# A Fourier transform and two feed-forward layers on one core: layer 1 begins with two token blocks on a quarter of its weights, and the weight conversion changes form

## The chip, the cores and the metric

The program runs on one core of one Trainium2 chip, in one launch. Its engines are TensorE (PE; PEld is its weight load), VectorE (DVE), ScalarE (ACT), GpSimd (POOL) and SyncE (SP, which here only issues DMAs). The metric is device time in microseconds; less is better.

## The reference, cut to what matters

```python
batch, seq, dim = (4, 3008, 256)          # x: float32
n_tokens, d_model, d_ff = (12032, 256, 2048)  # weights float32

X = np.fft.fft(x, axis=1); X = np.fft.fft(X, axis=2); x1 = X.real
h = x1 @ w_in          # layer 1
g = np.maximum(h, 0.0) ** 2
x2 = g @ w_out
h = x2 @ w_in2         # layer 2
y = (h * np.cos(h)) @ w_out2
```

The weights reach the kernel as 8-byte floats (they are drawn and then scaled in double precision), so each must be turned into two 12-bit-rounded float32 parts, "hi" and "lo".

## The kernel before, in words

Every matmul is done in three products of the two parts (hi by hi, hi by lo, lo by hi), so a stationary 128x128 tile meets 512 moving columns three times. The transform uses symmetries: tokens are handled in 6020 pairs, 1505 per batch; the pairs of all batches stand in one row and are cut into 12 blocks of 512 (the last has 388). A batch's input comes in three pieces of rows (`load_x`), each of which is **folded**: sums and differences on VectorE (`fold_a`, `fold_eo`, `fold_b`), then split into hi (`fold_hi`, ScalarE) and lo (`fold_lo`). `transform` multiplies the folded rows with tables of sines and cosines (six pieces, loaded once, kept to the end of the transforms), in four jobs per batch (cos and sin, part 0 and part 1); `finish` adds and splits the result and stores it to DRAM as z. The Fourier transform along the other axis is multiplied into `w_in` (`dft_w1`, `split_w1`).

**Layer 1** goes block by block; a block has 16 steps, one for each tile f of 128 of the 2048 hidden units. In a step TensorE makes h (`l1_mm1`, L462, 6 matmuls), VectorE makes s = sum and difference of the pair (`l1_add`, L469 and two of L215), ScalarE does relu, square and the hi part (`l1_act`, L479 to L482), GpSimd the lo part gl (`l1_lo`, L490, two halves), and three steps later TensorE adds to the block's result in PSUM (`l1_mm2`, L502, 12 matmuls). h has two PSUM tiles; the result of a block takes two more (acc), which `l1_out` empties after the 16th step. **Layer 2** (L535 to L586) does the same kind of work in 24 half blocks of 8 steps.

**Conversions.** `from_f64` works on 128 x 512 weights: two 32-bit words each. In the window of layer 1's first block there are 14 of them: six for `w_in` (pieces (1,0) to (3,1); a chunk of two gives four tiles f) and eight for `w_out` (keys 0, 2, ... 14, two tiles f each). Each has on VectorE a mask (L164), a merge (L167), a rest (L170), a guarded hi part (L180) and a power (L183). In ten of them ("shared", by the table `SHARED`) ScalarE and GpSimd make the lo part (L175, L188 on GpSimd); in the other four two more instructions on VectorE do (L177, L190). 16 conversions for layer 2's weights run late in layer 1, all on VectorE.

The first batch's input is folded and its part 0 transformed before layer 1; part 1 in its first steps. Layer 1's first block needs a new chunk of `w_in` every four steps and a new key of `w_out` every two. Batch 1 is folded in steps 11 to 24 and its z is needed by block 2, which reaches into batch 1, at step 32. x pieces of batches 1 to 3 go through the buffers A and B, which `l1_out` also uses.

**Order.** Each call is put into a list with a time in steps (`Order.at`), which the table `TIMES` may replace by name; the list is sorted and issued. An engine runs its instructions in that order and waits for semaphores; nothing is reordered on the chip. `FOLDS` says which of batch 0's first and last fold operations run on GpSimd ("P").

Of the kernel before, what the change touches and what calls it, by code (L numbers as in the profile page):

```python
# [89 lines left out]
def kernel(ctx: ExitStack, tc: tile.TileContext, x, x128, cs, tab0, tab1, w_in1, w_out1, w_in2, w_out2, out):  # L90
# [530 lines left out]
    def convert(t, key, st, fn, steps=(-0.5, 0, 0, 0)):  # L621
# [3 lines left out]
        def start():  # L625
            got.extend(fn(shared))
            for g in got[:4]:
                g()
# [253 lines left out]
```

## Time and profile before

| | |
|---|---|
| median of three runs | 1972.07 us (1969.3 to 1972.27) |
| the profiled execution | 1969.98 us, span 1968.2 us |
| busy share of the span | PE 96%, ACT 75%, DVE 72%, POOL 56% |
| layer 1's first step / 25th step / 49th step begins | 41.6 / 197.8 / 313.6 us |
| layer 2's first step begins | 928.5 us |

The profiled execution spends 1.8 us outside its span. Times in rows count from the span's start. A group of rows by line gives the busy time of all its instructions, the mean of one, and the idle time of the engine just before them with what ended it. `x12` is a count.

### The profile page before, as it was taken

How to read it: one execution, taken by the hardware profiler on the slowest of the kernel's cores; microseconds unless marked ns; L12 is line 12 of the kernel's file. 1: busy time of each engine (PE TensorE's matmuls, PEld its weight loads, DVE VectorE, ACT ScalarE, POOL GpSimd, SP SyncE). 2: the span in 40 equal slices, each digit the busy share in tenths (PEclk: the TensorE clock that was granted, in tenths of full speed). 3: DMA queues.
4: the chain of work that ended last, by engine and by line, in shares of the span. 5: the costliest groups of instructions: out<-in, count | busy, mean ns of one | idle time of the engine just before them, and what ended most of it. 6: DMA issues, size and time to landing. Idle time of an engine off the chain costs nothing.

```text
span 1968.2 us, 23258 instructions
## 1 busy us (share of the span) xinstructions
PE 1896.0 (96%) x8544; PEld 1575.4 (80%) x8544; DVE 1424.7 (72%) x1558; ACT 1472.3 (75%) x1519; POOL 1093.3 (56%) x716
## 2 busy tenths in 40 slices
PE   5688999999999999999999999999999999999999
...
GB/s 250 96 91 86 90 113 65 82 56 107 49 93 126 81 145 112 130 64 173 117 33 46 51 33 33 33 33 32 33 63 35 33 33 33 32 33 34 58 27 17
DMA packets 64389, 140.17 MB, mean 71 GB/s; under 512 B 7680, under 2 KB 19088, under 8 KB 64276
## 3 DMA queue, kind: packets, MB, share of 16 engines
...
q8 instruction: 67, 1.10, 0.2%
...
## 4 chain that ended last, share of the span: by engine, by line
PE 66%; DVE 11%; ACT 4%; issue 2%; DMA 0%; DVEq 0%; POOL 0%; ACTq 0%
PE acc L586 26%; PE h L535 17%; PE acc L502 9%; PE acc L535 8%; PE h L462 4%; DVE s L215 4%; DVE u L469 2%; ACT s L480 1%; ACT s L479 1%; DVE cvh L180 1%; DVE f L177 1%; PE h L290 1%; DVE f L170 1%; DVE ol L215 1%; ACT gh L482 1%
## 5 line engine op out<-in xcount | busy, mean ns | idle before, releaser
L574 POOL TENSOR_TENSOR gl<-r,gh 128x1024 fp32r<-128x1024 f32 (+1 forms) x189 | 446.4, 2362 | 539.6 <-ACT gh L567 468.1
L490 POOL TENSOR_TENSOR gl<-s,gh 128x512 fp32r<-128x512 f32 (+1 forms) x384 | 515.8, 1365 | 247.8 <-ACT gh L482 213.5
L549 DVE SCALAR_TENSOR_TENSOR r<-n,h 128x1024 f32<-128x1024 int32 (+1 forms) x129 | 154.7, 1199 | 214.5 <-ACT n L541 214.5
L479 ACT ACTIVATE s<-s 128x1024 f32<-128x1024 f32 (+1 forms) x192 | 199.6, 1040 | 137.2 <-DVE s L215 133.4
L215 DVE TENSOR_TENSOR s<-u,h 128x512 f32<-128x512 f32 (+1 forms) x384 | 242.8, 674 | 28.7 <-POOL inB L328 2.8
L541 ACT ACTIVATE n<-h 128x1024 int32<-128x1024 f32 (+1 forms) x129 | 130.4, 1011 | 155.2 <-PE h L535 155.2
L502 PE MATMUL acc<-gh,wbh 128*128 128x512 f32 (+1 forms) x768 | 238.3, 392 | 1.6 <-DVE ol L215 1.6
L549 DVE SCALAR_TENSOR_TENSOR r<-n,r 128x1024 f32<-128x1024 int32 (+1 forms) x192 | 232.7, 1212 | 6.6
L502 PE MATMUL acc<-gh,wbl 128*128 128x512 f32 (+1 forms) x768 | 235.7, 388 | 0.0
L502 PE MATMUL acc<-gl,wbh 128*128 128x512 f32 (+1 forms) x768 | 234.8, 387 | 0.0
L469 DVE SCALAR_TENSOR_TENSOR u<-zb,wc,h 128x512 f32<-128x512 f32 (+1 forms) x192 | 140.3, 731 | 127.7 <-PE h L462 125.3
L557 ACT ACTIVATE r<-r,halfpi 128x1024 f32<-128x1024 f32 (+1 forms) x192 | 218.4, 1138 | 6.2
L480 ACT ACTIVATE s<-s 128x1024 f32<-128x1024 f32 (+1 forms) x192 | 200.6, 1045 | 6.1
L482 ACT ACTIVATE gh<-s 128x1024 fp32r<-128x1024 f32 (+1 forms) x192 | 200.6, 1045 | 6.1
L556 ACT ACTIVATE r<-r 128x1024 f32<-128x1024 f32 (+1 forms) x192 | 198.2, 1032 | 6.7 <-DVE r L549 6.7
L586 PE MATMUL acc<-gh,wbl 128*128 128x512 f32 (+1 forms) x768 | 202.0, 385 | 0.0
L586 PE MATMUL acc<-gh,wbh 128*128 128x512 f32 (+1 forms) x768 | 202.0, 385 | 0.0
L586 PE MATMUL acc<-gl,wbh 128*128 128x512 f32 (+1 forms) x768 | 202.0, 385 | 0.0
L535 PE MATMUL h<-xh,wah 128*128 128x512 f32 (+1 forms) x516 | 198.8, 385 | 3.0 <-issue 1.5
L535 PE MATMUL h<-xl,wah 128*128 128x512 f32 (+1 forms) x516 | 198.5, 385 | 0.0
L535 PE MATMUL h<-xh,wal 128*128 128x512 f32 (+1 forms) x516 | 198.5, 385 | 0.0
L567 ACT ACTIVATE gh<-r 128x1024 fp32r<-128x1024 f32 (+1 forms) x192 | 197.1, 1027 | 0.3 <-DVE r L215 0.3
...
## 6 DMA issues: line engine op xcount, KB each, us to landing
...
```

What stands on the lines that cost most here:

```text
L215: nc.vector.tensor_tensor(out=out, in0=in0, in1=in1, op=op)
L479: nc.scalar.activation(s[:, :, :w], s[:, :, :w], AF.Relu)
L480: nc.scalar.activation(s[:, :, :w], s[:, :, :w], AF.Square)
L482: nc.scalar.activation(hi[:, :, :w], s[:, :, :w], AF.Copy)
L490: nc.gpsimd.tensor_tensor(out=lo[:, n, :w], in0=s[:, n, :w], in1=f32(hi)[:, n, :w], op=ALU.subtract)
L502: nc.tensor.matmul(accs[1, k][m][:, n, :w], wt, g[:, n, :w], start=f == 0 and i == 0, stop=f == NF - 1 and i == 2)
L535: nc.tensor.matmul(a[:, j, :w], st, mv[:, m, :w], start=m == 0 and q == 0, stop=m == 1 and q == 2)
L549: nc.vector.scalar_tensor_tensor(out=r[:, :, :w], in0=n[:, :, :w], scalar=-c, in1=src[:, :, :w], op0=ALU.mult, op1=ALU.add)
L556: nc.scalar.activation(r[:, :, :w], r[:, :, :w], AF.Abs)
L557: nc.scalar.activation(r[:, :, :w], r[:, :, :w], AF.Sin, bias=halfpi, scale=-1.0)
L574: e.tensor_tensor(out=lo[:, :, :w], in0=r[:, :, :w], in1=f32(hi)[:, :, :w], op=ALU.subtract)
L586: nc.tensor.matmul(accs[2, k][:, m, :w], w_out_t([c[part] for c in wo2], f, m), g[:, j, :w], start=f == 0 and q == 0, stop=f == NF - 1 and ...
```

## The change

The 1504 first pairs of a batch make three blocks of their own (512, 512, 480; the last batch 512, 512, 484), so that blocks follow batches. Layer 1 runs in **phases**: block 0 with tiles f 0 to 3, block 1 with f 0 to 3, block 2 with all 16, then block 1 and block 0 with f 4 to 15, then the others whole. After a phase that is cut short ScalarE copies the PSUM sums (`l1_part`), they go to DRAM, and come back (`load_part`) to be added in `l1_out`. Batch 1's z is needed at step 48 instead of 32, and its folding stands behind the conversions; x pieces of batches 1 to 3 are staged in the buffers of the tables, which are therefore loaded again for each batch (`reload_tab`, six pieces, GpSimd's DMA queue).

A conversion reads the same weights a second time, shifted by two bytes (`load_mid`, or in `load_cv`), so that the middle bits come out in a word of their own. `from_f64` then has on VectorE a guard (L171), a mask (L175), a merge (L179), a rest (L187 or L189), a power (L183) and the lo part (L196), ScalarE takes the absolute value before and the hi part after the merge, and nothing runs on GpSimd; the four earliest conversions read no shifted copy and keep a join (L192). Every step of a conversion or fold has its own time. Batch 0's fold is all on VectorE, its quarter sums moved behind part 0's transforms. Layer 2's conversions begin at step 101 (110 before), five steps each (four before). `TIMES` is a new table of 488 entries.

```diff
-BLOCKS = [(c, min(BLK, NPAIR - c)) for c in range(0, NPAIR, BLK)]
+BLOCKS = [(JB // 16 * 16 * b + c, min(BLK, (NPAIR - JB // 16 * 16 * b if b == B - 1 else JB // 16 * 16) - c))
+          for b in range(B) for c in range(0, JB, BLK)]
 NB = len(BLOCKS)
+PHASES = [(0, 0, FCH), (1, 0, FCH), (2, 0, NF), (1, FCH, NF), (0, FCH, NF)] + [(k, 0, NF) for k in range(3, NB)]
+SEQ = [(k, f) for k, f0, f1 in PHASES for f in range(f0, f1)]
...
-SHARED = {(3, 1): False, (2, 1): False, 0: False, 8: True, (0, 1): False, (0, 0): True, 4: True, (1, 1): False, (1, 0): True}
-FOLDS = {(2, 1): 'P', (0, 0): 'P', (0, 1): 'P', (1, 1): 'P', (1, 0): 'D', (2, 0): 'D'}
...
+FOLDS = {}
...
+    def shifted_in(w, k, col, n):
+        return w.bitcast(I16)[k * P:(k + 1) * P, 4 * col + 1:4 * (col + n) - 1]
+    def shifted_out(w, f, n):
+        return w.bitcast(I16)[f * P:(f + n) * P, 1:4 * D - 1].rearrange("(f p) m -> p f m", p=P)
...
+        def size():
+            got["a"] = buf("f64t", "f64t", I32, fft, 1, (P, BLK)) if sh is None else other
+            nc.scalar.activation(got["a"].bitcast(F32), w1.bitcast(F32), AF.Abs)
+        def guard():
+            a = got["a"].bitcast(F32)
+            v.tensor_scalar(out=a, in0=a, scalar1=TINY, scalar2=None, op0=ALU.max)
...
         def merge():
-            v.scalar_tensor_tensor(out=got["a"], in0=w1, scalar=-0x40000000, in1=got["a"], op0=ALU.bitwise_and, op1=ALU.bitwise_or)
+            a = got["a"]
+            v.scalar_tensor_tensor(out=a, in0=w1, scalar=-0x40000000, in1=a, op0=ALU.bitwise_and, op1=ALU.bitwise_or)
+            nc.scalar.activation(hi, a.bitcast(F32), AF.Copy)
...
+        def power():
+            v.tensor_scalar(out=got["a"], in0=got["a"], scalar1=-0x800000, scalar2=None, op0=ALU.bitwise_and)
 
...
-            v.tensor_scalar(out=w1, in0=w1, scalar1=0x1FF, scalar2=None, op0=ALU.bitwise_and)
+            if middle is None:
+                v.tensor_scalar(out=w1, in0=w1, scalar1=0x1FF, scalar2=None, op0=ALU.bitwise_and)
+            else:
+                v.tensor_scalar(out=middle, in0=middle, scalar1=0x1FFFFFF, scalar2=None, op0=ALU.bitwise_and)
...
-        def upper_part():
-            v.scalar_tensor_tensor(out=hi, in0=sizes.pop(key), scalar=SMALLEST, in1=got["a"].bitcast(F32), op0=ALU.is_ge, op1=ALU.mult)
-
-        def power():
-            v.tensor_scalar(out=got["a"], in0=hi.bitcast(I32), scalar1=-0x800000, scalar2=None, op0=ALU.bitwise_and)
-
...
+            r, unit = (w1.bitcast(F32), 2.0 ** -20) if middle is None else (middle, 2.0 ** -36)
+            v.scalar_tensor_tensor(out=lo, in0=r, scalar=unit, in1=got["a"].bitcast(F32), op0=ALU.mult, op1=ALU.mult)
+        return [size, guard, mask, merge, rest, power] + [join] * (middle is None) + [lower]
...
+    def reload_tab(i, t):
+        tabs[i][t] = buf(f"t{i}{t}", f"t{i}{t}", F32R, fft, 1, (P, 2, TW[i]))
+        load_tab(i, t)
...
+        return [mirrored] + [lambda i=i, fn=fn: fn(i) for fn, i in (
+            (eo, 0), (eo, 1), (half, 0), (half, 1), (hi, 0), (lo, 0), (quarter, 0), (quarter, 1), (hi, 1), (lo, 1))]
...
+    def load_mid(key, tag):
+        t = buf(tag, "mid", I32, fft, 1, (P, 2, TW[int(tag[1])])).rearrange("p h n -> p (h n)")
+        sh = t[:, :2 * BLK]
+        spare[key] = sh.rearrange("p (n t) -> p n t", t=2),
+        if isinstance(key, tuple):
+            c, k = key
+            nc.sync.dma_start(out=sh.bitcast(I16)[:, :4 * BLK - 2], in_=shifted_in(w_in1, k, c * FCH * P, BLK))
+        else:
+            nc.sync.dma_start(out=sh.bitcast(I16).rearrange("p (f n) -> p f n", f=2)[:, :, :4 * D - 2], in_=shifted_out(w_out1, key, 2))
...
+    def l1_part(k, m):
+        c, w = BLOCKS[k]
+        s = buf(f"t{m}{k}", "part", F32, fft, 1, (P, 2, TW[m]))[:, :, :BLK]
+        nc.scalar.activation(s[:, :, :w], accs[1, k][m][:, :, :w], AF.Copy)
+        part_dram[k, m] = dram.tile([P, 2 * BLK], F32, name=f"part{k}{m}")
+        nc.sync.dma_start(out=part_dram[k, m].rearrange("p (n w) -> p n w", n=2)[:, :, :w], in_=s[:, :, :w])
+    def load_part(k, m):
+        w = BLOCKS[k][1]
+        parts[k, m] = buf(f"{'BA'[m]}1", "ol", F32R)
+        nc.sync.dma_start(out=f32(parts[k, m])[:, :, :w], in_=part_dram[k, m].rearrange("p (n w) -> p n w", n=2)[:, :, :w])
 
     def l1_out(k, m):
...
-        tt(lo[:, :, :w], a[:, :, :w], f32(hi)[:, :, :w], ALU.subtract)
+        src = accs[1, k][m][:, :, :w]
+        hi = buf(f"{'BA'[m]}0", "oh", F32R)[:, :, :w]
+        if (k, m) in parts:
+            lo = parts.pop((k, m))[:, :, :w]
+            tt(f32(lo), src, f32(lo), ALU.add)
+            src = f32(lo)
+        else:
...
+    def staged(t):
+        return [buf(f"t{j // NT}{j % NT}", "inT", F32, fft, 1, (P, 2, TW[j // NT])).rearrange("p h n -> p (h n)")[:, :2 * BLK]
+                .rearrange("p (h n) -> p h n", h=2) for j in (2 * t, 2 * t + 1)]
...
+    KEYS = (0, 2, (1, 0), (1, 1), 4, (2, 0), (2, 1), 6, 8, (3, 0), (3, 1), 10, 12, 14)
+    t = 0.4
+    for n, key in enumerate(KEYS):
+        if n >= 2:
+            at(n * 1.5 - 1, lambda key=key, tag=f"t{n % 2}2": load_mid(key, tag), ("load_mid", key))
...
+            for t in range(NT):
+                at(start + gap * ((i * NT + t) // 2 + 1) + 0.1, lambda i=i, t=t: reload_tab(i, t), ("tab", b, i, t))
         for i, job in enumerate(JOBS):
-            def start(b=b, job=job):
+            def begin(b=b, job=job):
                 jobs[b, job] = ps_h.tile([P, 2, BLK], F32, name="h")
                 transform(job, jobs[b, job], lhs_of(b), P)
 
...
+    begins, i = {}, 0
+    for n, (k, f0, f1) in enumerate(PHASES):
+        begins[n] = i
+        if n == 1:
+            at(2.5, lambda k=k: load_zb(k, first["x"][1]), ("load_z", n))
+        elif n == 2:
+            at(4.2, lambda k=k: load_z(k), ("load_z", n))
+        elif n > 2 and PHASES[n - 2][0] != k:
+            at(max(i - 5.1, begins[n - 1] + 0.2), lambda k=k: load_z(k), ("load_z", n))
...
+            at(i + LAG + (1.25 if f == f0 else 0.3), lambda k=k, f=f, b=f == f0, e=f == f1 - 1: l1_mm2(k, f, b, e), ("mm2", i))
+            i += 1
         for m in range(2):
-            at(NF * (k + 1) + LAG - 0.55, lambda k=k, m=m: l1_out(k, m), ("out", k, m))
+            if f1 < NF:
+                at(i + LAG - 0.55, lambda k=k, m=m: l1_part(k, m), ("part", k, m))
+            else:
+                at(i + LAG - 0.55, lambda k=k, m=m: l1_out(k, m), ("out", k, m))
+                if f0:
+                    at(i + LAG - 2, lambda k=k, m=m: load_part(k, m), ("load_part", k, m))
 
     def open_late():
         fft_ctx.close()
...
```

Line numbers of the changed kernel follow in the rows below. **VectorE, the conversion of one pair of w_out tiles** early in layer 1: `wo` is the loaded weight, `mid` the shifted copy, `u` and `s` belong to `l1_add`, wbh and wbl are hi and lo. Before, a shared one (the lo part stands on GpSimd):

```order
L164 TENSOR_SCALAR f64t<-wo 128x512
L167 SCALAR_TENSOR_TENSOR f64t<-wo,f64t 128x512
L170 TENSOR_SCALAR wo<-wo 128x512
L469 SCALAR_TENSOR_TENSOR u_625<-zb,wc_96,h 128x512
L215 TENSOR_TENSOR s<-u_625,h 128x512 x2
L180 SCALAR_TENSOR_TENSOR wbh<-size,f64t 128x512
L183 TENSOR_SCALAR f64t<-wbh 128x512
```

and of the changed kernel, its steps after the guard:

```order
L175 TENSOR_SCALAR mid<-mid 128x512
L224 TENSOR_TENSOR wal<-h,wah 128x1024
L179 SCALAR_TENSOR_TENSOR mid<-wo,mid 128x512
L189 TENSOR_SCALAR mid<-mid 128x512
L536 SCALAR_TENSOR_TENSOR u_747<-zb,wc_96,h 128x512
L224 TENSOR_TENSOR s<-u_747,h 128x512 x2
L183 TENSOR_SCALAR mid<-mid 128x512
L196 SCALAR_TENSOR_TENSOR wbl<-mid 128x512
```

The hi part has left VectorE, the lo part has come to it, and one of the layer's `l1_add` groups stands between.

**VectorE, where batch 1's folding begins**: `inB` (before) and `inT` (now) are x pieces. Before, in the middle of the conversions:

```order
L469 SCALAR_TENSOR_TENSOR u_944<-zb,wc_96,h 128x512
L215 TENSOR_TENSOR s<-u_944,h 128x512 x2
L224 TENSOR_TENSOR inB_885<-inB_885,inB_886 128x1024
L164 TENSOR_SCALAR f64t<-wo 128x512
L167 SCALAR_TENSOR_TENSOR f64t<-wo,f64t 128x512
L170 TENSOR_SCALAR wo<-wo 128x512
L469 SCALAR_TENSOR_TENSOR u_1023<-zb,wc_96,h 128x512
L215 TENSOR_TENSOR s<-u_1023,h 128x512 x2
```

and now, after the last lo part of the last conversion:

```order
L536 SCALAR_TENSOR_TENSOR u_1443<-zb,wc_96,h 128x512
L224 TENSOR_TENSOR s<-u_1443,h 128x512 x2
L189 TENSOR_SCALAR mid<-mid 128x512
L183 TENSOR_SCALAR mid<-mid 128x512
L196 SCALAR_TENSOR_TENSOR wbl<-mid 128x512
L250 TENSOR_TENSOR inT<-inT 128x1024
L536 SCALAR_TENSOR_TENSOR u_1490<-zb,wc_96,h 128x512
L224 TENSOR_TENSOR s<-u_1490,h 128x512 x2
L224 TENSOR_TENSOR inT<-inT 128x512 x2
```

No fold of batch 1 now stands ahead of a conversion.

**GpSimd, the steps of the first blocks**: `gl` is `l1_lo`, wbl and wil the lo parts of weights, `t` a piece of the tables. Before:

```order
L175 TENSOR_TENSOR wo<-wo 128x512
L188 TENSOR_TENSOR wbl<-wo,f64t 128x512
L490 TENSOR_TENSOR gl<-s,gh 128x512 x2
L188 TENSOR_TENSOR wil<-inB_489,f64t 128x512
L490 TENSOR_TENSOR gl<-s,gh 128x512 x2
L175 TENSOR_TENSOR wo<-wo 128x512
L490 TENSOR_TENSOR gl<-s,gh 128x512 x2
L188 TENSOR_TENSOR wbl<-wo,f64t 128x512
```

and now, from the fifth step on:

```order
L557 TENSOR_TENSOR gl<-s,gh 128x512 x8
L557 TENSOR_TENSOR gl<-s,gh 128x480 x32
L557 TENSOR_TENSOR gl<-s,gh 128x512 x14
L207 DMA t_1727<-tab_in 128x1504
L519 DMA xh<-zh 128x2x512
```

The conversions' two operations are gone, and the first table piece to be loaded again stands behind 27 steps of `gl`.

## Rows read from the trace of the kernel before

**Rows 1.** Page, part 2: busy tenths in 40 slices of 49.2 us, TensorE.
```profile
PE   5688999999999999999999999999999999999999
```

**Rows 2.** Windows: length, busy per engine (instructions), clock, DMA share, GB/s.
```profile
41.60:197.80 156.20, 123.88 (x483) 95.19 (x482) 147.20 (x183) 102.82 (x118) 96.48 (x70) 0.86 0.29 94
197.80:313.60 115.80, 112.74 (x529) 92.20 (x527) 82.49 (x109) 82.41 (x85) 73.61 (x56) 0.99 0.30 95
313.60:928.50 614.90, 605.36 (x2784) 505.46 (x2785) 464.59 (x614) 487.27 (x494) 415.93 (x326) 1.00 0.31 101
928.50:1968.20 1039.70, 1032.63 (x4646) 866.67 (x4644) 697.14 (x605) 785.94 (x798) 485.32 (x245) 1.00 0.13 40
```

**Rows 3.** Chain of waits, 400 to 560 us: start, duration, work.
```profile
402.21 2.73 PE acc L502 x12
...
406.31 2.73 PE acc L502 x12
...
482.85 3.61 DMA inA<-x_in
...
546.69 3.28 PE h L290 x24
```

**Rows 4.** Groups by line, VectorE, 41.6 to 197.8 us: busy, mean ns, idle before.
```profile
L215 DVE TENSOR_TENSOR s<-u,h 128x512 f32<-128x512 f32 x46 | 29.6, 684 | 2.5 <-ACT size L150 0.5
L469 DVE SCALAR_TENSOR_TENSOR u<-zb,wc,h 128x512 f32<-128x512 f32 x23 | 17.0, 741 | 2.8 <-PE h L462 2.0 <-DMA wc<-wc 0.5
L215 DVE TENSOR_TENSOR inB<-inB 128x512 f32<-128x512 f32 (+1 forms) x12 | 13.4, 1161 | 0.1
L167 DVE SCALAR_TENSOR_TENSOR f64t<-wo,f64t 128x512 int32<-128x512 int32 x8 | 10.0, 1244 | 0.3
L180 DVE SCALAR_TENSOR_TENSOR wbh<-size,f64t 128x512 fp32r<-128x512 bf16 x8 | 8.7, 1092 | 0.0
...
L164 DVE TENSOR_SCALAR f64t<-wo 128x512 int32<-128x512 int32 x8 | 5.7, 717 | 0.0
...
L183 DVE TENSOR_SCALAR f64t<-wbh 128x512 int32<-128x512 int32 x8 | 5.1, 635 | 0.3
L177 DVE SCALAR_TENSOR_TENSOR inB<-inB 128x512 f32<-128x512 uint32 x3 | 4.9, 1642 | 0.1
...
L224 DVE TENSOR_TENSOR inB<-inB,inB 128x1024 f32<-128x1024 f32 x2 | 3.9, 1968 | 0.0
L215 DVE TENSOR_TENSOR wal<-h,wah 128x1024 fp32r<-128x1024 f32 x3 | 3.7, 1222 | 0.6 <-ACT wah L365 0.6
...
L258 DVE TENSOR_TENSOR dl<-inB,dh 128x512 fp32r<-128x512 f32 x4 | 2.7, 687 | 0.1
...
L190 DVE SCALAR_TENSOR_TENSOR wil<-inB,f64t 128x512 fp32r<-128x512 f32 x3 | 2.1, 693 | 0.2
```

**Rows 5.** Timeline of VectorE, front: start, duration, work, idle before.
```profile
35.53 1.10 DVE L215 TENSOR_TENSOR z<-z,h 4x376 f32<-4x376 f32 x2 [1.20 <-ACT z L297]
...
45.66 0.75 DVE L469 SCALAR_TENSOR_TENSOR u<-zb,wc,h 128x512 f32<-128x512 f32 x1 [0.55 <-DMA wc<-wc]
```

**Rows 6.** Timeline of VectorE, two equal merges.
```profile
59.98 2.18 DVE L167 SCALAR_TENSOR_TENSOR f64t<-wo,f64t 128x512 int32<-128x512 int32 x1
...
70.64 0.69 DVE L167 SCALAR_TENSOR_TENSOR f64t<-inB,f64t 128x512 int32<-128x512 int32 x1
```

**Rows 7.** Groups by line, GpSimd, 41.6 to 197.8 us.
```profile
L490 POOL TENSOR_TENSOR gl<-s,gh 128x512 fp32r<-128x512 f32 x45 | 65.2, 1472 | 19.5 <-ACT gh L482 18.8 <-PE acc L502 0.7
L188 POOL TENSOR_TENSOR wbl<-wo,f64t 128x512 fp32r<-128x512 f32 x7 | 10.2, 1459 | 4.2 <-DVE f64t L183 2.7 <-PE acc L502 1.4
L175 POOL TENSOR_TENSOR wo<-wo 128x512 f32<-128x512 f32 x7 | 8.0, 1143 | 15.6 <-ACT wo L174 15.6
```

**Rows 8.** Page, part 5: ScalarE's relu, one of three such passes.
```profile
L479 ACT ACTIVATE s<-s 128x1024 f32<-128x1024 f32 (+1 forms) x192 | 199.6, 1040 | 137.2 <-DVE s L215 133.4
```

**Rows 9.** DMA issues: tile, queue, count, KB each, median us to landing.
```profile
t<-tab_in POOLq DMA_DIRECT2D x3, 756.0 KB, 9.1
```

More of the change, by code (lines that the diff above doesn't have):

```diff
@@ L13 @@
 I32 = mybir.dt.int32
+I16 = mybir.dt.int16
 BF16 = mybir.dt.bfloat16
@@ L261, in load_128, with scratch @@
+    def scratch(*shape):
+        n = math.prod(shape)
+        if "at" not in first:
+            first["scratch"], first["at"] = buf("zb", "zb", bufs=2, shape=(P, BLK)), 0
+        first["at"] += n
+        names = "abcd"[:len(shape)]
+        return first["scratch"][:, first["at"] - n:first["at"]].rearrange(
+            f"p ({' '.join(names)}) -> p {' '.join(names)}", **dict(zip(names, shape)))
     def load_128():
-        raws["mid"] = buf("x128", "x128", F32, fft, 1, (P, 2, NT, 4, B))
+        raws["mid"] = scratch(2, NT, 4, B)
@@ L619, in start_first, with convert @@
         transform(job, first[job], lhs_of(0), P, ts)
-    def convert(t, key, st, fn, steps=(-0.5, 0, 0, 0)):
-        shared = SHARED.get(key, True)
+    def convert(t, span, key, fn):
         got = []
[L625 to L628, printed above, removed]
-        def middle():
-            for g in got[4:6]:
-                g()
-            if not shared:
-                got[6]()
-        def last():
-            if shared:
-                got[6]()
-        at(t + steps[0], lambda: size_f64(key, st(), shared=shared), ("size", key))
-        for i, f in enumerate((start, middle, last)):
-            at(t + steps[1 + i], f, ("conv", key, i))
@@ new lines, in convert, with fold, step @@
+        for j in range(8):
+            at(t + span * (j - 1) / 7, lambda j=j: step(j), ("conv", key, j))
+    def fold(times, b, t):
+        got = []
+        def step(j):
+            if j == 0:
+                got.extend(fold_steps(b, t))
+            got[j]()
+        for j, when in enumerate(times):
+            at(when, lambda j=j: step(j), ("fold", b, t, j))
+    at(-91, load_128, "load_128")
+    at(-90, lambda: load_w1(0, pair("A", I32)), ("load_w1", 0))
+    at(-89, lambda: load_x(0, 0, pair("B")), ("load_x", 0, 0))
@@ new lines @@
+    for b, (load, start, gap, t1, gap1) in {1: ((14, 21, 21.6), 26, 4, 38.4, 1.5), 2: ((53, 53.5, 54), 54, 4.6, 68, 2), 3: ((76, 76.5, 77), 78, 4.6, 92, 2)}.items():
+        for t in range(NT):
+            at(load[t], lambda b=b, t=t: load_x(b, t, staged(t)), ("load_x", b, t))
+            fold([start + gap * t + gap / 11 * j for j in range(11)], b, t)
+        for i in range(2):
+            for t in range(NT):
+                at(start + gap * ((i * NT + t) // 2 + 1) + 0.1, lambda i=i, t=t: reload_tab(i, t), ("tab", b, i, t))
@@ new lines @@
+            finish(t1 + gap1 * i + 0.9, b, job, lambda b=b, job=job: jobs[b, job], lambda: pair("B", F32R), 0.3)
+    begins, i = {}, 0
[7 more added lines that the diff above has]
+            at(max(i - 5.1, begins[n - 1] + 0.2), lambda k=k: load_z(k), ("load_z", n))
+        for f in range(f0, f1):
```

329 lines of the change are left out of this document (157 added, 172 removed).

## The prediction

> **What bounds the kernel now.** I read the slices first: TensorE is busy 9 tenths or more from the fourth slice on and only 5 to 8 tenths in the first three, about 150 us [rows 1]. The windows then cut the span where layer 1's steps 0, 24 and 48 and layer 2 begin [rows 2]. The chain of waits gives TensorE's pace when nothing holds it: 12 matmuls of a second product take 2.73 us, and two such groups begin 4.10 us apart (402.21 and 406.31), which is one step with its 6 matmuls for h; a transform job takes 3.28 us [rows 3]. Set against that pace, the windows lose: steps 0 to 24 need 24 x 4.10 = 98.4, three weight transforms of 12 matmuls (8.2) and the first batch's part 1 (about 8.6), together 115, and take 156.2, so 41 us are lost. Steps 24 to 48 need 24 x 4.10 + 4 x 3.28 = 111.5 and take 115.8: 4.3 lost. Steps 48 to 192 need 128 x 4.10, 16 steps of 388 columns (16 x 4.10 x 388/512 = 49.7) and 8 jobs (26.2), in all 600.7, and take 614.9: 14.2 lost. Layer 2 has TensorE at 1032.6 of 1039.7.
>
> In the window that loses 41 us, VectorE is busy 147.2 of 156.2 us (94%) and TensorE 123.9, at a granted clock of 0.86, mostly its upper level of 2.4 GHz with stretches at 1.2 [rows 2]. VectorE is the bound there. It does 24 groups of `l1_add` (0.741 + 2 x 0.684 = 2.11 us each), 14 conversions and nearly three folds [rows 4].
>
> **Steps 0 to 24.** The conversions first, with means of this window [rows 4]. A single-input operation is 0.676 (mean of 0.717 and 0.635), a merge 1.244, the hi part 1.092, a join 1.642, a lo part 0.693. A shared conversion costs VectorE 3 x 0.676 + 1.244 + 1.092 = 4.36, ten of them 43.6; an unshared one 1.642 + 0.693 more, 6.70, four of them 26.8: 70.4 together. Now a shifted one has four single-input operations, a merge and a lo part. For that lo part the rows lie between 0.693 and 1.642; I take 1.092, the row that is nearest in kind (two SBUF inputs, in the same queue): 5.04, twelve of them 60.5, and two with a join 13.4: 73.9. So the conversions give VectorE nothing, they add 3.5 us.
>
> What leaves is the folding. A fold costs 1.968 + 6 x 1.161 + 2 x 0.687 = 10.3 us [rows 4]; two and about six tenths of batch 1's three stand in the window: 26.8 us, all moved behind the last conversion. Block 0's two `l1_out` subtractions leave as well (2 x 1.22, priced as wal, of the same shape): in their place four PSUM copies go to ScalarE, about 1.04 each [rows 8], on an engine busy 102.8 of 156.2. Sixteen of the 24 steps are 480 wide, which takes 32/512 of 16 x 2.11 = 2.1 off. VectorE's sum is 147.2 + 3.5 - 26.8 - 2.4 - 2.1 = 119.4.
>
> TensorE's own need is 8 x 4.10 + 16 x 4.10 x 480/512 + 8.2 + 8.6 = 111, so VectorE still decides, by less. Before, it was busy 94% of the time. Each conversion now waits for ScalarE twice (the absolute value ahead of the guard; the hi part, whose input the power overwrites), and ScalarE's queue holds groups of three passes of 1.04 us [rows 8]; for that I take 92%, bounds 96% and 80%. 119.4/0.92 = 129.8 instead of 156.2: **26.4 us won**. The two blocks ahead matter here as cover: tiles 0 to 3 serve twelve steps rather than four, so TensorE is not held by a chunk that is not yet converted; that lets VectorE's queue set the pace without a second bound.
>
> One price in this sum hangs on GpSimd. The same merge took 0.69 us at 70.64 and 2.18 at 59.98 [rows 6]. GpSimd was busy 96.5 us of the window, of it 18.2 in the seven shared conversions of `w_out` (10.2 and 8.0), and three of `w_in` besides, about 8 by the same means [rows 7]; that leaves it about 70 us of 130, a share of 54% after 62%. I keep the slowed means, because `l1_lo`, 1.47 us twice a step, stays.
> The Trainium skill ("SBUF — State Buffer", section "Who interferes with whom") has a rule for it: a VectorE operation with two SBUF inputs and a GpSimd operation exclude each other for a whole instruction, by which starts first. The trace agrees with 0.69 against 2.18. By the rule the price is not the share of GpSimd's time but whether its operations begin ahead of conversions, which the new order could avoid; that is the first rival.
>
> **The start.** One addition and five lo parts of batch 0's fold come from GpSimd to VectorE; six quarter sums and three lo parts go behind part 0's transforms. At about 0.7 us for 512 columns alone [rows 6] these nearly cancel (4.9 against 4.2), and contention with GpSimd goes. But the first `l1_add` waits for the 128th column's sums, made at 35.53 to 36.6, stored and broadcast back: it begins at 45.66, 9.0 later [rows 5], and that path is unchanged. I take 0, bounds -4 and +3.
>
> **Steps 24 to 48.** Here the folds arrive: VectorE has 24 x 2.11 + 3 x 10.3 + 4 sums of z at 1.10 [rows 5] + six passes of 1.22 for the results of blocks 2 and 1 (block 1's with the added partial sums) = 93.2, 84% of TensorE's 111.5, after 82.5 of 115.8 (71%) [rows 2]. The work fits beside TensorE, spread singly between `l1_add` groups. I take a loss of 5 instead of 4.3: **+0.7**, bounds 0 and +8. If the cover goes, what is late next is batch 1's z.
>
> **Steps 48 to 192.** Six blocks of 512, two of 480, one of 484: 96 x 4.10 + 32 x 3.84 + 16 x 3.88 + 26.2 = 604.8, 4.1 more than before only because the narrow blocks have moved. Of the 14.2 lost, the chain names a load of x as a piece of 3.61 us at 482.85 [rows 3], in a buffer shared with `l1_out`; x is now staged in table buffers, so I take those 3.6 off: 615.4, **+0.5**. The 16 late conversions have two two-input passes instead of four and a fifth step of time; they lie beside a full TensorE, so nothing is counted, with -5 as bound. The 18 reloads of tables and the shifted loads are hidden in my sum: a table piece took 9.1 us to land in the crowded front [rows 9], and shifted loads of two thirds of that size stand about two or more steps ahead. The reloads' cover is weighed below.
>
> **Layer 2.** The same columns and matmuls. The last half is 484 wide instead of 388; the passes behind the last products grow by 24% of about 0.8 (1.04 for 1024 columns [rows 8]), six of them: **+1**, bounds 0 and +3.
>
> **Sum.** -26.4 + 0 + 0.7 + 0.5 + 1 = -24.2 against the profiled execution's 1969.98 (span 1968.2 and 1.8 around it; the median is 1972.07, 0.1% above): 1945.8, so **1946 us**.
>
> **Rivals.** *Contention goes with GpSimd's share.* For: 26 us of its work leave, and conversions stand between `l1_add` groups, which read PSUM. Against: its two halves of `l1_lo` fill more than half of each step. If the two-input passes ran at 0.69: 14 x 0.55 + 14 x 0.40 + 2 x 0.95 = 15.2 off, 104.2/0.92 = 113, just above TensorE's 111: 16.5 more won, **1929**.
>
> *ScalarE holds the conversions.* For: 28 waits on a queue with groups of 3.1 us. Against: ScalarE is busy 66%, and other VectorE work stands between merge and power. At a quarter of a group each, 28 x 0.78 = 22 less the 3 that the 92% contains: **1965**.
>
> *Slower: the tables come too late.* Place: the last two pieces of part 1 in batches 1 to 3. Each load waits on GpSimd's queue until a fold has left the buffer, with `l1_lo` queued behind it and TensorE's second products behind that; the pieces stand some two steps (8.2 us) and one job (3.28) ahead of the transform that reads them. Two landings in a row at 9.1 are 18.2 against 11.5: TensorE waits 6.7; six waits of one `l1_lo` half (1.5) are 9 more. Three batches: 47 us, **1993**. It decides from 8 us a batch on. For: the fold is the busiest stretch of VectorE. Against: 9.1 was measured with the front's loads beside it, and later windows have the DMA engines busy only 0.30 [rows 2].
>
> **Chances.** Forecast 0.56, contention 0.21, ScalarE 0.13, tables 0.08, others 0.02. Range 1929 to 1965: from the first rival to the second. A measurement of this kernel can tell about 0.2%, 3.9 us: the second rival lies about on that edge (a third of it counts as no change). Faster 0.86, no change 0.05, slower 0.09.
>
> **What would show it.** Step 24 beginning near 171 us (197.8 before), step 48 near 289 (313.6), layer 2's first step near 904; VectorE busy 91 to 93% until step 24 and no fold of batch 1 in it; a shifted conversion near 5 us on VectorE; TensorE losing under 6 us from step 24 to 48. Wrong would be: VectorE idle before guard or power with ScalarE as releaser (second rival), means of merge and lo part near 0.7 (first), a transform of batch 1 to 3 waiting for a table (third), or steps 24 to 48 over 120 us, which would give back what the moved folds won.

## The result, and the profile after

The changed kernel takes 1954.55 us (median of 4 runs, 1953.09 to 1955.47); the kernel before took 1972.17 beside it (4 runs, 1969.3 to 1975.4). The ratio is 0.991, 95% interval 0.9892 to 0.9927: faster by 17.6 us, where 26 were forecast (1946, range 1929 to 1965). In the profiled executions the span went from 1968.2 to 1952.0, 16.2 less, and the parts below sum to that.

The slices of the page after, TensorE and its granted clock, answer [rows 1]: where TensorE stood at 5, 6 and 8 tenths it now has 6, 8 and 8.
```profile
PE   6889999999999999999999999999999999999999
...
PEclk8999999999999999999999999999999999999999
```

The windows after, cut at the same steps (0, 24, 48 and layer 2), in the columns of [rows 2]:
```profile
35.50:166.00 130.50, 114.64 (x504) 90.37 (x505) 116.78 (x179) 98.78 (x121) 66.07 (x53) 0.92 0.51 163
166.00:283.00 117.00, 112.40 (x529) 92.39 (x528) 89.48 (x118) 89.34 (x94) 82.24 (x66) 0.99 0.45 146
283.00:906.50 623.50, 614.43 (x2786) 508.58 (x2785) 484.90 (x618) 498.05 (x511) 422.05 (x336) 0.99 0.40 132
906.50:1952.00 1045.50, 1038.92 (x4645) 870.82 (x4643) 697.80 (x605) 786.32 (x798) 484.27 (x245) 1.00 0.13 40
```

Set beside [rows 2], each part against its forecast:

| Part | before | after | change | forecast |
|---|---|---|---|---|
| until step 0 | 41.6 | 35.5 | -6.1 | 0 (-4 to +3) |
| steps 0 to 24 | 156.2 | 130.5 | -25.7 | -26.4 |
| steps 24 to 48 | 115.8 | 117.0 | +1.2 | +0.7 |
| steps 48 to 192 | 614.9 | 623.5 | +8.6 | +0.5 |
| layer 2 | 1039.7 | 1045.5 | +5.8 | +1 (0 to +3) |

The two terms between step 0 and step 48 came out near their forecasts. The total is near the forecast only because the first error and the last two have opposite signs. Most of the experiments below are about those three.

The border at step 0 moved too. Before, one transform of part 1 (38.45 to 41.62) ran ahead of step 0 on TensorE; now all of part 1 stands behind it (from 42.25 on), and so do nine operations of VectorE. So the first two rows belong together: from the start to step 24 the change is -31.8 us, where -26.4 were forecast.
```profile
38.45 1.14 PE L290 MATMUL acc<-t,dh 128*128 128x188 f32 x4
...
41.62 0.50 PE L462 MATMUL h<-xh,wah 128*128 128x512 f32 x1
```

In the front after, step 0's first matmul and VectorE's first `l1_add`, the second answering [rows 5]: step 0 is 6.1 earlier, `l1_add` (45.66 before) only 2.8, and it no longer waits for a DMA.
```profile
35.45 0.49 PE L529 MATMUL h<-xh,wah 128*128 128x512 f32 x1 [1.54 <-ACT xh L382]
...
42.82 0.74 DVE L536 SCALAR_TENSOR_TENSOR u<-zb,wc,h 128x512 f32<-128x512 f32 x1
```

VectorE's groups by line in steps 0 to 24 answer [rows 4, 6] (busy, mean ns, idle before):
```profile
L224 DVE TENSOR_TENSOR s<-u,h 128x480 f32<-128x480 f32 (+1 forms) x47 | 29.2, 661 | 2.7 <-POOL zl L383 0.6
L536 DVE SCALAR_TENSOR_TENSOR u<-zb,wc,h 128x480 f32<-128x480 f32 (+1 forms) x24 | 17.2, 716 | 0.7 <-PE h L529 0.6
L189 DVE TENSOR_SCALAR mid<-mid 128x512 int32<-128x512 int32 x11 | 10.4, 944 | 0.0
L175 DVE TENSOR_SCALAR mid<-mid 128x512 int32<-128x512 int32 x12 | 8.4, 700 | 0.2
L183 DVE TENSOR_SCALAR mid<-mid 128x512 int32<-128x512 int32 x11 | 8.4, 763 | 2.6 <-ACT wbh L180 1.6 <-ACT wih L180 1.0
L171 DVE TENSOR_SCALAR mid<-mid 128x512 f32<-128x512 f32 x12 | 7.1, 592 | 0.8 <-ACT mid L167 0.8
L196 DVE SCALAR_TENSOR_TENSOR wil<-mid 128x512 fp32r<-128x512 int32 x6 | 6.0, 1004 | 0.1
...
L179 DVE SCALAR_TENSOR_TENSOR mid<-inB,mid 128x512 int32<-128x512 int32 x6 | 4.6, 774 | 0.1
```
A shifted conversion is the sum of its six means, 0.592 + 0.700 + 0.73 + 0.763 + 0.944 + 0.98 = 4.7 us (forecast 5.04; two of the means are of two tiles each), and no sum of batch 1 (`inT`) is in the stretch. Its parts moved more than the sum: a merge takes 0.73 instead of the 1.244 priced, the four single-input passes 3.00 instead of 2.70. By the rows of all conversions, these fell from 69.0 to 63.4 us in the stretch, where the forecast had 3.5 more, and the nine operations of batch 0, which the forecast of VectorE's sum left out, bring 5.0 (`in` and `inB`). ScalarE is named for 2.6 + 0.8 us of VectorE's idle time in the shifted conversions, so the second rival did not come. GpSimd has 57.8 us of `l1_lo` where [rows 7] had 65.2, and none of the conversions:
```profile
L557 POOL TENSOR_TENSOR gl<-s,gh 128x480 fp32r<-128x480 f32 (+1 forms) x43 | 57.8, 1367 | 60.0 <-ACT gh L549 42.8 <-issue 12.1 <-PE h L417 4.6
```
What TensorE waited for in steps 0 to 24 (total, times, longest), before and after:
```profile
PE h L462 <- DVE s L215: 11.4, 7, 2.7
PE h L358 <- DVE wih L180: 8.3, 3, 3.5
PE h L462 <- ACT wcrow L368: 7.9, 1, 7.9
...
PE h L529 <- DVE s L224: 4.9, 3, 3.8
PE h L417 <- DVE wil L196: 3.8, 3, 2.2
```
Of 32.4 us of waits before, 19.1 were for the next converted chunk of `w_in` (wih, wil, wcrow); of 17.1 after, 4.8 are.

A table piece lands in 6.1 or 5.3 us, against the 9.1 of [rows 9], and no transform of batches 1 to 3 waits for one; the third rival did not come either.
```profile
t<-tab_in POOLq DMA_DIRECT2D x12, 756.0 KB, 6.1
t<-tab_in POOLq DMA_DIRECT2D x12, 752.0 KB, 5.3
```

### The profile page after: what moved, and what is told of

The parts are those of the page before. It is cut to its first block, busy times and chain, and to the rows that moved or that the text cites. A ratio compares the mean times of both kernels' runs of the same rounds, so it can differ in the third digit from the quotient of the medians.

```text
span 1952.0 us, 23443 instructions
## 1 busy us (share of the span) xinstructions
PE 1898.9 (97%) x8544; PEld 1574.4 (81%) x8544; DVE 1413.7 (72%) x1563; ACT 1481.9 (76%) x1537; POOL 1059.7 (54%) x709
## 3 DMA queue, kind: packets, MB, share of 16 engines
q1 hardware_dynamic: 50692, 108.32, 16.2%
## 4 chain that ended last, share of the span: by engine, by line
PE 75%; DVE 4%; ACT 1%; issue 1%; DVEq 0%; ACTq 0%
PE acc L672 26%; PE h L621 17%; PE acc L569 15%; PE acc L621 9%; PE h L529 7%; DVE inT L224 1%; DVE s L224 1%; PE h L312 1%; DVE r L635 1%; DVE u L536 1%; ACT s L547 0%; ACT s L546 0%; DVE ol L224 0%; DVE inT L250 0%; DVE r L224 0%
## 5 line engine op out<-in xcount | busy, mean ns | idle before, releaser
L660 POOL TENSOR_TENSOR gl<-r,gh 128x1024 fp32r<-128x1024 f32 (+2 forms) x189 | 445.2, 2355 | 543.2 <-ACT gh L653 471.0
L557 POOL TENSOR_TENSOR gl<-s,gh 128x512 fp32r<-128x512 f32 (+2 forms) x384 | 514.2, 1361 | 288.8 <-ACT gh L549 251.6
L546 ACT ACTIVATE s<-s 128x1024 f32<-128x1024 f32 (+2 forms) x192 | 199.6, 1039 | 113.6 <-DVE s L224 112.4
L224 DVE TENSOR_TENSOR s<-u,h 128x512 f32<-128x512 f32 (+2 forms) x384 | 242.4, 673 | 23.4 <-DVE u L536 1.4
L569 PE MATMUL acc<-gh,wbh 128*128 128x512 f32 (+2 forms) x768 | 239.0, 393 | 0.3 <-DVE ol L224 0.3
L635 DVE SCALAR_TENSOR_TENSOR r<-n,r 128x1024 f32<-128x1024 int32 (+2 forms) x192 | 232.9, 1213 | 6.6
L569 PE MATMUL acc<-gl,wbh 128*128 128x512 f32 (+2 forms) x768 | 236.0, 388 | 1.0 <-POOL gl L557 0.9
L569 PE MATMUL acc<-gh,wbl 128*128 128x512 f32 (+2 forms) x768 | 235.6, 388 | 0.0
L643 ACT ACTIVATE r<-r,halfpi 128x1024 f32<-128x1024 f32 (+2 forms) x192 | 218.3, 1137 | 6.2
L547 ACT ACTIVATE s<-s 128x1024 f32<-128x1024 f32 (+2 forms) x192 | 200.5, 1044 | 6.1
L549 ACT ACTIVATE gh<-s 128x1024 fp32r<-128x1024 f32 (+2 forms) x192 | 200.5, 1044 | 6.1
L672 PE MATMUL acc<-gh,wbh 128*128 128x512 f32 (+2 forms) x768 | 202.8, 386 | 0.0
L672 PE MATMUL acc<-gh,wbl 128*128 128x512 f32 (+2 forms) x768 | 202.8, 386 | 0.0
L672 PE MATMUL acc<-gl,wbh 128*128 128x512 f32 (+2 forms) x768 | 202.8, 386 | 0.0
```

The lines of the kernel that those rows point to most:

```text
L224: nc.vector.tensor_tensor(out=out, in0=in0, in1=in1, op=op)
L546: nc.scalar.activation(s[:, :, :w], s[:, :, :w], AF.Relu)
L547: nc.scalar.activation(s[:, :, :w], s[:, :, :w], AF.Square)
L549: nc.scalar.activation(hi[:, :, :w], s[:, :, :w], AF.Copy)
L557: nc.gpsimd.tensor_tensor(out=lo[:, n, :w], in0=s[:, n, :w], in1=f32(hi)[:, n, :w], op=ALU.subtract)
L569: nc.tensor.matmul(accs[1, k][m][:, n, :w], wt, g[:, n, :w], start=begin and i == 0, stop=end and i == 2)
```

## The experiments

Medians are compared with the 1954.55 of the changed kernel or with the kernel before, which ran beside each; step times come from the profiled execution, where the kernel before has 313.6 and the changed kernel 283.0 for step 48.

### Block widths: three runs

The places where the forecast failed late are layer 2, with no other change in it than its columns, and steps 48 to 192. First layer 2's steps after, on TensorE: two of 512 columns in a row and two of 480 (start, duration).
```profile
1004.38 0.39 PE L621 MATMUL h<-xh,wah 128*128 128x512 f32 x1
...
1009.82 0.39 PE L621 MATMUL acc<-xh,wah 128*128 128x512 f32 x1
...
1101.82 0.38 PE L621 MATMUL h<-xh,wah 128*128 128x480 f32 x1
...
1107.02 0.37 PE L621 MATMUL acc<-xh,wah 128*128 128x480 f32 x1
```
A step of 512 takes 5.44 us, one of 480 takes 5.20, where 480/512 of the former is 5.10. TensorE does not idle in either.

**The kernel before with the new widths alone.**
```
-BLOCKS = [(c, min(BLK, NPAIR - c)) for c in range(0, NPAIR, BLK)]
+BLOCKS = [(JB // 16 * 16 * b + c, min(BLK, ...)) for b in range(B) for c in range(0, JB, BLK)]
```


> The kernel before with one part of the change alone: its blocks are 512, 512, 480 per batch (484 at the end) instead of eleven of 512 and one of 388; the number of columns and of matmuls stays. Theory W (a narrow matmul costs more than its share of columns): in the changed kernel's trace a layer 2 step of 480 columns takes 5.23 us where 480/512 of 5.425 is 5.09, a layer 1 step 3.92 where 3.84 is the share. Six halves of 8 steps and three blocks of 16 make 6 x 8 x 0.14 + 3 x 16 x 0.08 = 10.6, with the 484 against the 388 about 11, less what lies in the first 48 steps where TensorE waits anyway: 8 to 11 us slower, 1980 to 1983, five to six of them in layer 2. Rival P (time goes by columns, as the prediction had it; the change's loss sits in its waits): within 2 us of the kernel before, 1972, and layer 2 at 1040 to 1041.

Measured: 1981.7 us, ratio to before 1.0048 (1.0034 to 1.0062). Layer 2 takes 1045.4, as in the changed kernel:
```profile
934.80:1980.20 1045.40, 1038.97 (x4645) 871.07 (x4643) 697.83 (x605) 786.34 (x798) 484.33 (x245) 1.00 0.13 40
```
Steps 48 to 192 take 623.2 (311.6 to 934.8), 8.3 more than before. W holds: the widths alone cost 5.7 us in layer 2, of the 5.8 there, and 8.3 in steps 48 to 192. That the latter is near the changed kernel's 8.6 is chance: here all but 0.4 of it stands behind step 80 (474.2 us, 466.3 before), in the changed kernel 6.0 of it in steps 48 to 80, where every block is 512 wide.

**Matmuls alone.**


> Matmuls alone, 72 of each of 19 widths from 512 to 376 columns, each with its own weight load, nothing beside them; it computes nothing of the reference. Theory W: the time from one matmul to the next is 0.226 at 512, 0.218 at 480 and 0.177 us at 388, as in the two kernels, so 512 is out of line with its neighbours or the widths just under it are; the widths between say where it begins. Rival P: 0.226 at 512 and 0.212 at 480, straight in the columns: then the narrow steps of the kernels wait for something beside them.

ScalarE reads each result of 12 matmuls, so the distance of its starts is the time of 12. Its timeline, for 480 and 512 columns (the second column is ScalarE's own duration):
```profile
331.44 0.97 ACT L67 ACTIVATE o<-w 128x960 f32<-128x960 f32 x1 [1.57 <-PE w L66]
334.04 0.97 ACT L67 ACTIVATE o<-w 128x960 f32<-128x960 f32 x1 [1.63 <-PE w L66]
...
362.60 1.03 ACT L67 ACTIVATE o<-w 128x1024 f32<-128x1024 f32 x1 [1.69 <-PE w L66]
365.32 1.03 ACT L67 ACTIVATE o<-w 128x1024 f32<-128x1024 f32 x1 [1.69 <-PE w L66]
```
2.60 and 2.72 for 12: 216.7 ns a matmul at 480 columns, 226.7 at 512; at 388 it is 2.12, 176.7 ns. Others read the same way: 226.7 at 504, 223.3 at 500 and 496, 220 at 488, 213.3 at 472, 180 at 400. So narrowing from 512 to 504 gives nothing, and 32 columns fewer give 10 ns, not the 14 of their share. W holds with only ScalarE's reads beside TensorE; why the time goes in such stairs stays open.
The Trainium skill's page "TensorE: Matmul & The Clock Gate", section "Back-to-back issue gap", gives columns at 2.4 GHz plus 2.5 ns for an isolated matmul, an estimate of 216 and 202.5 ns for 512 and 480, and about 131 ns at 512 for a stream of weight loads and matmuls; the run's 226.7 and 216.7 decide.

**The changed kernel with blocks of 512 again behind batch 0.**
```
+START = [0, 512, 1024] + list(range(JB // 16 * 16, NPAIR, BLK))
+BLOCKS = [(c, min(d, NPAIR) - c) for c, d in zip(START, START[1:] + [NPAIR])]
```


> The changed kernel with blocks of 512 again behind batch 0: 512, 512, 480, then eight of 512 and one of 420. Theory W: two blocks of 480 and their four halves become 512, and 484 becomes 420; by the measured steps layer 1 gains about 2.7 us and layer 2 about 5, so 1946 to 1949 against 1954.6. Rival P: within 2 us of 1954.6.

Measured: 1946.3 us, ratio to before 0.987 (0.9855 to 0.9884), 8.2 under the changed kernel. Layer 2 is back at 1040.0 (904.3 to 1944.3). This is the fastest version of the whole work that ran, and the batches' borders, which the change follows in every block, are not needed behind batch 0.

### Steps 48 to 80: what holds TensorE while batch 2 is folded

In steps 48 to 192 TensorE is idle 9.1 us after (before 9.5), but 7.2 of them in steps 48 to 80, where it had 3.5 before. These steps, before and after:
```profile
313.60:462.20 148.60, 145.13 (x673) 119.79 (x674) 80.48 (x117) 113.58 (x114) 93.60 (x74) 0.99 0.20 67
283.00:437.60 154.60, 147.36 (x673) 118.84 (x671) 115.47 (x139) 109.56 (x111) 97.73 (x77) 0.99 0.39 135
```
VectorE has 35 us more there. Before, batch 2 was folded in steps 37 to 49, so about 5 us of folds stood in these steps; now some 45 us do, batch 2's and the first of batch 3. Two windows of 10 us after show where TensorE loses, each with a mean granted clock under 1.00, its upper level of 2.4 GHz:
```profile
363.00:373.00 10.00, 7.32 (x27) 5.25 (x26) 9.71 (x13) 9.18 (x11) 6.03 (x5) 0.88 0.44 162
433.00:443.00 10.00, 7.69 (x28) 5.92 (x27) 8.49 (x11) 5.22 (x6) 3.22 (x3) 0.83 0.11 36
```
VectorE is the busy engine in the first, so my first thought was too many folds in too few steps.

**Batch 2's folds spread, from step 47.**
```
-('fold', 2, 0, 0): 54.15, ... ('fold', 2, 2, 10): 67.5
+('fold', 2, t, j): 47.1 + 6.5 * t + 6.5 * j / 11, ('load_x', 2, 0): 45.2
```


> The changed kernel with batch 2's three folds spread over steps 47 to 66.5 instead of 54 to 67.5, its loads of x from step 45 on; nothing else moves. Theory V (TensorE's losses between steps 59 and 80, 6.9 us idle with two stretches at the lower clock, come from a VectorE with three folds, l1_add and z sums in too few steps): the idle time up to the transforms, about 5 us, and 1.7 of the clock go: 1948 to 1951. Rival S (they come from VectorE's waits for ScalarE's queue, at the hi part of each fold and at the z sums, whose number stays): 1953 to 1955.

Measured: 1957.06 us, ratio 0.9921 (0.9907 to 0.9934): nothing won. The first fold waited for its x, with `l1_add` queued behind it:
```profile
288.31 1.23 DVE L250 TENSOR_TENSOR inT<-inT 128x1024 f32<-128x1024 f32 x1 [8.39 <-DMA inT<-x_in]
```
This cost 8 us between steps 48 and 56 and hid the answer (steps 56 to 80 took 114.3 us instead of 121.1). So it was made again with the folds behind the loads.

**Spread from step 51, with the wide blocks.**
```
+('fold', 2, t, j): 51.0 + 5.3 * t + 5.3 * j / 11, ('load_x', 2, 0): 45.2
```


> The wide blocks of the run with eight blocks of 512 behind batch 0, together with batch 2's folds spread over steps 51 to 66.5, their loads of x from step 45 on, so that the first fold does not wait for x as it did in the first spread (8.4 us, with l1_add behind it). Theory V (too many folds in too few steps): 3 to 6 us under the wide blocks alone, 1940 to 1943. Rival S (hand-offs to ScalarE's queue at each fold, whose number stays): 1945 to 1947.

Measured: 1953.58 us, ratio 0.9905 (0.9891 to 0.9918), 7 slower than the wide blocks alone. Both theories fall: V forecast a gain, S no change. Steps 48 to 80 take 162.2 us against 154.6. The folds' lo parts now take 1.60 us each and wait 8.8 for ScalarE (6.8 us in six and 2.4 in the changed kernel):
```profile
L224 DVE TENSOR_TENSOR dl<-inT,dh 128x512 fp32r<-128x512 f32 x6 | 9.6, 1602 | 8.8 <-ACT dh L266 8.8
```
That points at where a fold's operations stand rather than at how many share a step; no run separates the two. A closer look at the changed kernel's timeline showed this, GpSimd, VectorE and TensorE together:
```profile
334.76 1.29 POOL L557 TENSOR_TENSOR gl<-s,gh 128x512 fp32r<-128x512 f32 x1 [0.65 <-ACT gh L549]
334.93 1.67 DVE L224 TENSOR_TENSOR inT<-inT 128x512 f32<-128x512 f32 x1
...
338.34 0.69 DVE L224 TENSOR_TENSOR inT<-inT 128x512 f32<-128x512 f32 x1
...
342.84 0.50 PE L529 MATMUL h<-xh,wah 128*128 128x512 f32 x1 [0.65 <-DVE s L224]
```
Of four sums in a row, three begin just behind a half of `l1_lo` and take 1.67, 1.79 and 1.78 us; the third begins beside none and takes 0.69. `l1_add` stands behind them, and TensorE waits for that; all its waits that the trace lists in steps 48 to 80 are for `l1_add`'s s. The sums of this stretch (283 to 440):
```profile
L224 DVE TENSOR_TENSOR inT<-inT 128x512 f32<-128x512 f32 x16 | 25.1, 1601 | 0.1
L250 DVE TENSOR_TENSOR inT<-inT 128x1024 f32<-128x1024 f32 x4 | 7.8, 1955 | 0.3 <-DMA inT<-x_in 0.3
L224 DVE TENSOR_TENSOR dl<-inT,dh 128x512 fp32r<-128x512 f32 x6 | 6.8, 1130 | 2.4 <-ACT dh L266 2.4
```

**The changed kernel without `l1_lo` in steps 47 to 79.**
```
+        if 47 <= SEQ.index((k, f)) < 80:
+            gs[1, k, f] = hi, hi
+            return
```


> The changed kernel without l1_lo in steps 47 to 79, where batch 2 is folded: the second products take hi in the place of lo there, which leaves the lo part of these products out. It asks what holds TensorE between steps 59 and 80, since spreading the folds took nothing away. Theory L (the folds' sums collide with l1_lo: 1.60 us for one of 128x512 here, 1.15 in the kernel before, 0.66 in the front without GpSimd's work, so that three folds cost VectorE about 40 us): the sums fall to 0.7, the folds to 9.5 us each, and most of the 9.1 idle and 3.4 of clock go: step 80 begins 8 to 11 us earlier, near 428. Rival S (the waits are hand-offs to ScalarE, at the hi parts of a fold and at the z sums): under 3 us earlier.

One run: 1938.63 us; step 80 begins at 426.0 instead of 437.6. The window from step 48 on, and the same sums in it:
```profile
283.00:427.00 144.00, 143.99 (x675) 118.76 (x675) 97.62 (x143) 112.56 (x116) 13.90 (x14) 1.00 0.41 145
```
```profile
L224 DVE TENSOR_TENSOR inT<-inT 128x512 f32<-128x512 f32 x16 | 12.0, 788 | 0.1
L250 DVE TENSOR_TENSOR inT<-inT 128x1024 f32<-128x1024 f32 x4 | 4.9, 1220 | 0.4 <-DMA inT<-x_in 0.4
```
TensorE's idle time is gone, all of it, and the clock stays at its upper level. Theory L holds: the folds' operations collide with `l1_lo`, 1.60 us for a sum against 0.79, and this makes TensorE wait. Nothing else on VectorE changed as much: `l1_add`'s means are 0.74 and 0.68 us with `l1_lo` and without it, and TensorE has no listed wait for `l1_lo` itself in these steps.
By the rule of the Trainium skill that the prediction weighed ("SBUF — State Buffer", section "Who interferes with whom") this is an exclusive lock, and which engine begins first decides; the trace agrees, with 1.67 to 1.79 us for the sums that began behind a half of `l1_lo` and 0.69 for the one that did not.

**The first sum of each fold on GpSimd, wide blocks.**
```
-FOLDS = {}
+FOLDS = {(b, t): "P" for b in (2, 3) for t in range(3)}
```


> The wide blocks (eight of 512 behind batch 0) with the first sum of each fold of batches 2 and 3, 128x1024, on GpSimd. Theory L: it takes a collided 1.95 us from VectorE six times, but GpSimd's own sum, some 3 us by its l1_lo halves of 1.35 to 1.47, excludes VectorE's two-input operations too and holds l1_lo up; I expect 1944 to 1949 against 1946.3, no change. Rival V (VectorE's sum alone decides there): 3 to 6 us faster, 1940 to 1943.

Measured: 1967.32 us, ratio 0.9972 (0.996 to 0.9984), 21 slower than the wide blocks: worse than either theory. Steps 48 to 80 take 166.6 us against 154.6; 4.6 of the 21 stand ahead of step 48, where the edit moves nothing, and stay open. GpSimd's sum takes 2.45 us, but it stands in a queue behind `l1_lo`, and VectorE, which must go on with the fold, waits 19.3 us for it:
```profile
L224 DVE TENSOR_TENSOR inT<-inT 128x512 f32<-128x512 f32 x14 | 19.4, 1424 | 19.4 <-POOL inT L250 19.3
```

### The first 24 steps and the front

**One fold of batch 1 back among the conversions.**
```
-('fold', 1, 0, 0): 25.15, ... ('fold', 1, 0, 10): 29.85, ('load_x', 1, 0): 13.48
+('fold', 1, 0, j): 13.6 + j, ('load_x', 1, 0): 10.6
```


> The changed kernel with one of batch 1's three folds put back among the conversions (steps 13.6 to 23.6 instead of 25.2 to 29.9; its load of x from step 10.6). Theory V (VectorE sets the pace to step 24, so what it does there is paid, and behind step 24 the same work is hidden): the fold's 10.3 us at the 89.5% that VectorE is busy there make step 24 begin 11 us later, steps 24 to 48 give 1 to 4 back (4.6 us of TensorE's time are lost there): 1961 to 1965. Rival C (the 25.7 us came from the two blocks ahead, which keep TensorE supplied, and the folds were not the price): step 24 moves by under 3 us, 1953 to 1957.

Measured: 1962.55 us, ratio 0.9948 (0.9936 to 0.9961), 8.0 slower. Step 24 begins 6.4 later. The windows of steps 0 to 24 and 24 to 48:
```profile
35.40:172.40 137.00, 117.64 (x505) 93.29 (x505) 122.61 (x184) 99.39 (x122) 65.47 (x53) 0.90 0.48 155
172.40:291.90 119.50, 113.15 (x530) 92.71 (x529) 88.00 (x113) 89.75 (x93) 81.33 (x66) 0.97 0.44 143
```
VectorE has 5.8 us more and pays for it in full at its 89.5%, so C falls as it was put (under 3 us), and V holds for steps 0 to 24: what VectorE does there is paid. V's size was too large, since a fold costs only some 7 us there by its rows. At 6.4 us each, the 2.6 folds that left make some 17 of the 25.7 us, an estimate from this run; the conversions' lower rows stand beside them, and how much the two blocks ahead add, with which TensorE waits less for `w_in`, no run tells. And V was wrong behind step 24: nothing came back, these steps took 2.5 us more, at a clock of 0.97 instead of 0.99.

**Nine sums back in the front.**
```
+('fold', 0, t, 7 to 10): ahead of ('T', 0, i, t) again   # in words
```


> The changed kernel with the six quarter sums and three lo parts of batch 0's folds back ahead of part 0's transforms; everything else stays. Theory F (step 0 began 6.1 us earlier than before because VectorE's chain ahead of the transforms got shorter by these nine operations, 6 x 0.41 + 3 x 0.69 = 4.5 us by the changed kernel's rows): step 0 begins 3 to 4.5 later, at 38.5 to 40, and most of it stays to the end: 1957 to 1959. Rival G (the gain is that GpSimd no longer folds beside VectorE, which stretched VectorE's operations, and VectorE's 10.7 us of gaps before step 0 take the nine): step 0 moves by under 1.5 us, 1954 to 1956.

Measured: 1956.6 us, ratio 0.9919 (0.9906 to 0.9933). Step 0 begins at 39.16, 3.7 later, and 3.0 of it remain at the end of the profiled span (1955.0):
```profile
39.16 0.76 PE L529 MATMUL h<-xh,wah 128*128 128x512 f32 x1 [2.21 <-ACT xh L382]
```
F holds for 3.7 of the 6.1 us (three hi parts on ScalarE moved with the nine). The medians differ by only 2.0, under F's 1957 to 1959. The other 2.4 were not isolated. The rows name two candidates: the transform of part 1 that no longer stands ahead of step 0, and eight sums of the front that took 1.20 us each before, when GpSimd did part of the folds, and take 0.69 now (four of the eight before, and all eight after):
```profile
L215 DVE TENSOR_TENSOR inA<-inA 128x512 f32<-128x512 f32 x4 | 4.6, 1194 | 0.0
...
L224 DVE TENSOR_TENSOR in<-in 128x512 f32<-128x512 f32 x8 | 5.2, 688 | 0.1
```

**No `l1_lo` in steps 0 to 24.**
```
+        if SEQ.index((k, f)) < 24:
+            gs[1, k, f] = hi, hi
+            return
```


> The changed kernel without l1_lo in the first 24 steps: the second products take hi in the place of lo there, so the lo part of these products is left out, and GpSimd has nothing to do but its few lo parts of z. It measures what GpSimd's work costs VectorE. If contention makes the prices (first rival of the prediction): the two-input operations of the conversions and the masks fall to 0.69 and 0.43, a conversion from 4.7 to 3.35 us, VectorE's sum by 12 x 1.35 = 16 and step 24 begins 10 to 16 us earlier, at 150 to 156. If the prices are the operations' own: step 24 moves by under 3 us, and only waits of TensorE for lo go.

One run: 1939.84 us; step 24 begins at 155.1, 10.9 earlier. The window, and one pass of the conversions (0.944 us with `l1_lo` beside it):
```profile
35.40:155.10 119.70, 110.29 (x504) 88.98 (x505) 99.74 (x180) 98.18 (x121) 8.28 (x10) 0.96 0.54 177
```
```profile
L189 DVE TENSOR_SCALAR mid<-mid 128x512 int32<-128x512 int32 x11 | 4.6, 422 | 0.0
```
VectorE's sum falls by 17 us (116.8 to 99.7), a conversion to 3.1 us (four passes at 0.42 to 0.43, two at 0.69); TensorE then has 110.3 of 119.7 and becomes the bound, as the prediction's 111 said. The contention is real and worth 11 us here, in one run; the change has taken it off the merges and left it on the rest.

## Why the prediction was right, and where it was not

- **Steps 0 to 24, forecast -26.4, measured -25.7: right in its mechanism, and in its number with some luck.** VectorE's sum was forecast at 119.4 and is 116.8; the share at 92% and is 89.5%: two errors that cancel. Putting back one fold made step 24 later by about what that fold cost, so the moved folds are the larger part of the gain. The sum held by terms that cancel as well: the conversions were to add 3.5 and took 5.6 off (1.9 of it only because the last one's end now lies behind step 24), and the nine operations moved behind the start added 5.0, for which the sum had no term. That the two blocks ahead are needed as cover was not tried.
- **Steps 24 to 48, +0.7, measured +1.2: right.** Batch 1's folds arrived on VectorE (89.5 us, forecast 93.2) and TensorE was idle 4.6. What the prediction did not say is that batch 2's folds, some 31 us here before, left this stretch for steps 48 to 80.
- **The start, 0, measured -6.1, beyond its bound of -4: mis-sized.** The step that failed is "At about 0.7 us for 512 columns alone these nearly cancel (4.9 against 4.2)". The 4.2 held: the nine operations are worth 3.7, as the run that put them back shows. The 4.9 for what comes from GpSimd did not: VectorE is busy 24.8 us ahead of step 0 instead of 33.3, or 28.6 with the nine back, so that "contention with GpSimd goes", put at nothing, is by the rows worth some 4 us in eight sums alone. The second sentence failed as well. [rows 5] names the load of wc ahead of `l1_add`, not the 128th column; that column's sums are done at 36.6 now as before, and `l1_add` begins 6.2 us later without a wait, not 9.0. Where it does wait for them, with the nine back, it begins 5.1 us after them.
- **Steps 48 to 192, +0.5, measured +8.6: one term mis-sized, one missing.** "4.1 more than before only because the narrow blocks have moved" took a step's time as proportional to its columns. By measured steps (4.10, 3.92, 3.96, and 3.19 for the 388 before) the widths cost 96 x 4.10 + 32 x 3.92 + 16 x 3.96 less 128 x 4.10 + 16 x 3.19, 6.6 us, all behind step 80. "I take those 3.6 off" for the load of x held: behind step 80 TensorE is idle 1.8 us instead of 6.1, and the stretch is only 2.6 longer (468.9 against 466.3). The other 6.0 stand in steps 48 to 80, for which the prediction had no term: batch 2's folds moved there and collide with `l1_lo`. TensorE is idle 3.8 us more, and part of the rest went to the lower clock; without `l1_lo` these steps take 143.6 us.
- **Layer 2, +1 from its tail, measured +5.8: the wrong mechanism.** The same widths, by the same error: the kernel before with these widths alone has layer 2 at 1045.4. That "The same columns and matmuls" take the same time is false by 0.6%.
- **The rivals.** Contention going (1929) came for the merges alone (0.69 and 0.77): the lo parts at 1.00 and 0.94 are still above 0.69, single-input passes at up to 0.94 above 0.42, and the run without `l1_lo` shows the 11 us that were there to win, where the rival had 16.5. ScalarE's hand-offs cost 3.4 us of VectorE, inside the 89.5%. The tables were never late.
